# Two last stages of an attention and gated-layer kernel: an explicit order in place of a scheduler's

## The chip, the cores and the metric

The kernel runs on one core of a Trainium2 chip. The time is the device time of one execution in microseconds. Five engines work side by side, each through its own list of instructions: PE (the matrix engine; PEld is its loading of weights), DVE (vector), ACT (scalar), POOL (GpSimd) and SP (which issues DMA transfers). An instruction starts when its turn comes on its engine and what it waits for is there. PE writes its products into banks of an accumulator memory (PSUM), DVE and ACT read them from there.

## What is computed

```python
x = attention(q, k, v, cap)        # 4 x 12 heads, 448 tokens each: 1792 tokens x 768
h = ((x @ w1) * (x @ w2)) @ w3     # 1792 x 1024
x = h @ w_out                      # 1792 x 768
h = x @ w_in                       # 1792 x 1024
e = exp(h - max(h)); sm = e / (sum(e) + 1e-9)
solu = h * sm
ln = (solu - mean(solu)) / sqrt(var(solu) + 1e-6) * g_ln
out = ln @ w_out2                  # 1792 x 768
```

Everything is fp32, in and out.

## The kernel before

Attention comes first, then the gated stage. The plain products w3 · w_out · w_in are multiplied into one matrix W of 1024 x 1024 ahead of time, beside attention. So two matrix products are left behind the gated stage, and these are the two last stages: h = ab · W (ab are the gated values, kept in DRAM as `ab_dr`), and out = c · w_out2, where c is the normalised layer, kept in DRAM as `c_dr`, and g_ln is already multiplied into the weights.

Each stage goes over 7 pairs of 128-token tiles. For a pair and the weights cut into 2 x 2 blocks, seven block products take the place of eight, with sums of the blocks as operands; their order is 1, 2, 6, 7, 5, 4, 3. A product is 12 matmuls: 4 steps in depth times 3 terms, because every operand is kept as a rounded high part and a low part (`split`, L175: the high part is a cast on ACT, the low part a subtraction on DVE). A matmul is 512 columns wide in the first stage and 384 in the second.

The seven products of a pair go into three kinds of accumulator bank: u (two of them, in turn for successive pairs), y and v. Product 1 writes u, and its value is copied out (p1, ACT L774). Product 2 writes y, evicted with p1 added (DVE L781). Product 6 adds onto u, copied out (u2). Product 7 writes v, copied out (p7). Product 5 adds onto u, evicted with p7 added (L790). Product 4 adds onto v, evicted with u2 added (L793). Product 3 adds onto u, copied out by ACT (L795). So within a pair the third product needs the copy of the first, the fifth that of the third, the sixth that of the fourth, and the seventh the eviction behind the fifth.

Between the stages `solu` (L820 to 833) takes each tile of h through a maximum (DVE L823), an exponential with its sum (ACT L824), the weighting (DVE L827), squares with their sum (ACT L829), a power on POOL (L831) and the normalisation (DVE L832), and stores c. Behind it the second stage loads c again, transposed in blocks of 32 by the addresses of the DMA, turns it within the blocks (DVE L838, four times 512 a pair) and makes sums and operands of it (`turned_operands`, L840; x21 is a copy by ACT). The weights of the second stage are loaded into the place of the first stage's, behind their last products, and split in halves of 768 elements (`load_wg`, L868).

`ps`, `hp`, `op` and `conv` are pools; a tile with `bufs=n` has n places in turn, and a new tile waits until the one that had its place is no longer read. The order of instructions on each engine comes from the framework's scheduler, which works from estimated times; the loops at L875 to 915 say only what there is to do. The SoLU of the last pair is written behind the second pair of operands of the second stage.

Of the kernel before, what the change touches and what calls it, by code (L numbers as in the profile page):

```python
# [99 lines left out]
def attention_moe_solu(ctx: ExitStack, tc: tile.TileContext, q, k, v, cap, w12, w3t, wo, win, wout2, g_ln, out):  # L100
# [415 lines left out]
    def block_load(m, part, dr, t_dr, dst):  # L516
        sync.dma_start(out=raw(dst[:, 1, 2 * part:2 * part + 2, :]), in_=block_src(m, part, dr, t_dr))

    def block_split(dst, part):
        hi, lo = (dst[:, i, 2 * part:2 * part + 2, :] for i in range(2))  # L520
# [241 lines left out]
    NTT = NT // P  # L762
    PAIRS = NTT // 2

    def seven(n, a, wb, w, c1, c2, other):

        def product(bank, m, first):
            for k in range(NF // 2):
                for i, (x, e) in enumerate(THREE):
                    pe.matmul(bank, a[m][:, x, k * P:(k + 1) * P], wb[m][:, e, k, :], start=(first and k == 0 and i == 0), stop=(k == NF // 2 - 1 and i == 2), skip_group_check=not first)  # L770

        def kept(bank, name):
# [196 lines left out]
```

## Time and profile before

| | |
|---|---|
| device time, median of 3 runs | 824.34 us (822.47 to 825.29) |
| device time of the profiled execution | 828.39 us |
| its span, first to last instruction | 826.6 us |
| PE busy | 807.4 us, 98% |
| DVE busy | 604.3 us, 73% |
| ACT busy | 478.2 us, 58% |
| POOL busy | 74.8 us, 9% |
| first matmul of the two last stages | 574.75 us |

The profile is one execution, so sums are made against its own 828.39 us. A wait is written as idle time and the engine whose work ended it: `[1.02 <-ACT u L774]` behind a matmul means that PE stood still for 1.02 us until ACT's copy out of bank u at line 774 was done. Where several instructions of one line follow each other without a gap they stand as one (x12). PEclk is the granted clock of PE, 1.00 for full speed.

### The profile page before, as it was taken

How to read it: one execution, taken by the hardware profiler on the slowest of the kernel's cores; microseconds unless marked ns; L12 is line 12 of the kernel's file. 1: busy time of each engine (PE TensorE's matmuls, PEld its weight loads, DVE VectorE, ACT ScalarE, POOL GpSimd, SP SyncE). 2: the span in 40 equal slices, each digit the busy share in tenths (PEclk: the TensorE clock that was granted, in tenths of full speed). 3: DMA queues.
4: the chain of work that ended last, by engine and by line, in shares of the span. 5: the costliest groups of instructions: out<-in, count | busy, mean ns of one | idle time of the engine just before them, and what ended most of it. 6: DMA issues, size and time to landing. Idle time of an engine off the chain costs nothing. (4 is left out here: it accounts for less than half of the span.)

```text
span 826.6 us, 12057 instructions
## 1 busy us (share of the span) xinstructions
PE 807.4 (98%) x4251; PEld 676.4 (82%) x4251; DVE 604.3 (73%) x1076; ACT 478.2 (58%) x739; POOL 74.8 (9%) x147
## 2 busy tenths in 40 slices
PE   8999999999999999999989999999999999889998
PEld 4667888876777788888869999999888887789997
DVE  6999968788876687788746653332988889999851
ACT  6767868788677777777752301111655564754431
POOL 1110110110311221101111000000000000000000
PEclk9999999999999999999999999999999999889999
DMA  7878645577977445788546999971633349858411
GB/s 236 280 254 268 209 153 158 171 233 268 287 266 212 115 149 201 225 292 297 172 146 183 296 388 366 328 247 59 199 106 124 101 103 215 230 133 186 115 40 76
DMA packets 151292, 167.18 MB, mean 202 GB/s; under 512 B 71232, under 2 KB 124224, under 8 KB 149696
## 3 DMA queue, kind: packets, MB, share of 16 engines
q1 hardware_dynamic: 146240, 155.22, 59.0%
q0 software_dynamic: 4992, 11.19, 5.3%
q8 instruction: 33, 0.54, 0.3%
q14 instruction: 27, 0.22, 0.1%
HBM read 113.25 MB, written 47.53 MB: 195 GB/s over the span
## 5 line engine op out<-in xcount | busy, mean ns | idle before, releaser
L609 PE MATMUL ab<-xs,wt 128*128 128x448 f32 x1152 | 241.7, 367 | 0.4 <-ACT x L308 0.4
L609 PEld LDWEIGHTS ab<-xs,wt 128*128 128x128 f32 x1152 | 217.5, 189 | 20.6 <-ACT x L308 0.8
L259 ACT ACTIVATE sc<-sc,qscale 128x896 f32<-128x896 f32 (+1 forms) x96 | 84.9, 885 | 38.9 <-PE sc L251 28.6
L292 PE MATMUL o<-hi,v 128*66 128x448 f32 (+1 forms) x360 | 85.1, 371 | 1.8 <-ACT x L308 1.8
L260 ACT ACTIVATE p<-sc,capt 128x896 f32<-128x896 f32 (+1 forms) x96 | 85.6, 917 | 1.4
L770 PE MATMUL u<-ws,a 128*128 128x512 f32 x336 | 79.6, 390 | 1.0 <-ACT u L774 1.0
L380 PEld LDWEIGHTS f<-w,w_o 128*128 128x128 f32 x576 | 72.6, 190 | 9.4 <-issue 5.9
L380 PE MATMUL f<-w,w_o 128*128 128x256 f32 x576 | 78.4, 289 | 0.6 <-DVE w_o L177 0.6
L770 PEld LDWEIGHTS u<-ws,a 128*128 128x128 f32 x336 | 63.0, 188 | 14.3 <-ACT u L774 1.3
L275 DVE TENSOR_TENSOR lo<-p,hi 128x896 fp32r<-128x896 f32 x60 | 64.9, 1084 | 13.4 <-ACT hi L271 13.1
L398 PE MATMUL f<-w_i,w 128*128 128x512 f32 x288 | 70.1, 393 | 1.3 <-ACT w L176 1.0
L770 PE MATMUL u<-wg,c 128*128 128x384 f32 x336 | 64.3, 341 | 3.9 <-ACT h L795 3.9
L398 PEld LDWEIGHTS f<-w_i,w 128*128 128x128 f32 x288 | 53.7, 188 | 14.6 <-issue 1.5
L613 ACT COPY a<-ab 128x448 f32<-128x448 f32 x32 | 17.0, 532 | 82.9 <-PE ab L609 72.7
L770 PEld LDWEIGHTS u<-wg,c 128*128 128x128 f32 x336 | 60.3, 193 | 4.5 <-ACT h L795 4.2
L292 PEld LDWEIGHTS o<-hi,v 128*66 128x66 f32 (+1 forms) x360 | 39.1, 135 | 27.1 <-issue 8.8
L271 ACT CAST hi<-p 128x896 fp32r<-128x896 f32 x60 | 56.6, 948 | 0.4
L617 DVE TENSOR_TENSOR abs<-ab,a 128x448 f32<-128x448 f32 x32 | 19.8, 620 | 48.9 <-PE ab L609 36.5
L171 DVE SCALAR_TENSOR_TENSOR cv<-ld,cv 128x512 uint32<-128x512 uint32 (+1 forms) x80 | 51.9, 657 | 0.6
L172 DVE SCALAR_TENSOR_TENSOR cv<-ld,cv 128x512 uint32<-128x512 uint32 (+1 forms) x80 | 52.0, 656 | 0.6
L170 DVE TENSOR_SCALAR cv<-ld 128x512 uint32<-128x512 uint32 (+1 forms) x80 | 32.5, 410 | 20.5 <-DMA ld<-in_w 7.9
L309 POOL DMA_DIRECT2D xr<-x x48 | 25.6, 539 | 201.6 <-ACT x L308 194.5
(129 smaller groups left out, 1246.5 us busy)
## 6 DMA issues: line engine op xcount, KB each, us to landing
ld<-in_w SPq DMA_DIRECT2D x24, 512.0 KB, 5.0
w_dr<-wt SPq DMA_DIRECT2D x6, 1536.0 KB, 6.8
wt<-w_dr SPq DMA_DIRECT2D x6, 1536.0 KB, 8.4
ld<-in_w3t SPq DMA_DIRECT2D x16, 512.0 KB, 4.5
ab_dr<-abs SPq DMA_DIRECT2D x32, 224.0 KB, 4.9
ldab<-ab_dr SPq DMA_DIRECT2D x14, 512.0 KB, 4.0
c_dr<-e SPq DMA_DIRECT2D x14, 512.0 KB, 3.4
ldc<-c_dr SPq DMA_DIRECT2D x56, 128.0 KB, 3.3
```

The lines of the kernel that those rows point to most:

```text
L170: dve.tensor_scalar(x, hi, 5, 2, ALU.logical_shift_left, ALU.logical_shift_right)
L171: dve.scalar_tensor_tensor(x, hi, 0xC0000000, x, ALU.bitwise_and, ALU.bitwise_or)
L172: dve.scalar_tensor_tensor(x, lo, 29, x, ALU.logical_shift_right, ALU.bitwise_or)
L259: act.activation(sc[:, :w, :S], sc[:, :w, :S], AF.Tanh, scale=qscale)
L260: exp_[n, c] = act.activation(p, sc[:, :w, :S], AF.Exp, scale=capt)
L271: act.copy(hi, p)
L275: dve.tensor_tensor(lo, p, raw(hi), ALU.subtract)
L292: product_.append(pe.matmul(outs[n, j][:v_.shape[-1], :S], v_, t[rows, j if c < 3 else 0], **flags))
L380: pe.matmul(f[:, :QW], lw[:, a], rw[:, e], start=(g == 0 and m == 0), stop=(g == NF - 1 and m == 2))
L398: pe.matmul(f, w34[:, a, c, :], rw[:, e], start=(c == 0 and m == 0), stop=(c == NC - 1 and m == 2))
L609: pe.matmul(pp[f, b, i][:, :S], w[:, u], xs[b, c][:, e], start=(c == 0 and m == 0), stop=(c == NC - 1 and m == 2))
L770: pe.matmul(bank, a[m][:, x, k * P:(k + 1) * P], wb[m][:, e, k, :], start=(first and k == 0 and i == 0), stop=(k == NF // 2 - 1 and i == 2 ...
```

## The change

All of it is in the two last stages; in front of them the built program has the same instructions in the same order on every engine. The products, their order, their banks and their 12 matmuls stay. What is new:

- **The order.** Both stages are written under a mode in which the scheduler leaves the order alone. For pairs 0 to 13 (`r`; 0 to 6 are the first stage, 7 to 13 the second) and the seven products `j`, the program issues product (r, j), then the side work listed for the slot (r, j), then the eviction of product (r, j). Side work is listed by hand: operands, sums, transposes, SoLU's steps, weight splits, loads and stores.
- **Maxima in the evictions.** In the first stage the three evictions with a sum become one DVE instruction each that adds and takes a running maximum (L810), and product 3's copy moves from ACT to DVE and takes a maximum too (L830). SoLU's own pass for the maximum goes; a small negation (`top`, L836) is left.
- **Normalisation on ACT.** Instead of DVE's pass, an ACT pass with a scale and a shift per row (L859); POOL makes the shift with a second small product (L856).
- **Two low parts at once.** Operands 1 and 2, and 6 and 7, are cast and subtracted as one instruction of 1024 elements each (`two`), since their sources now lie beside each other. The transposes are 1024 wide as well, two a pair, into two banks each (L883).
- **Whole weights.** The second stage's weights are loaded and split as a whole (1536 elements), not in halves.
- **Places.** SoLU's last pair is spread over pairs 8 to 10. `early`, a pool that is closed ahead of the last stages, takes two tiles out of `conv`; `conv` and `op` hold four places for loads.

The core of the diff. The old functions that it removes are those printed above; of the lists of slots three lines stand here:

```diff
+    def at_slot(r, j, *todo):
+        side.setdefault((r, j), []).extend(todo)
...
+    def kept(r, g, name):
+        keeps[name] = hp.tile([P, HALF], F32, tag="kept", bufs=2, name=f"{name}_{r}")[:, :banks[g].shape[-1]]
+        act.copy(keeps[name], banks[g])
...
+    def added(r, i, half, g, keep):
+        w = banks[g].shape[-1]
+        dst = h[r][i][:, half * w:(half + 1) * w]
+        if r >= PAIRS:
+            dve.tensor_tensor(dst, banks[g], keeps[keep], ALU.add)
+            return
+        first = (i, half) in ((0, 0), (1, 1))
+        dve.tensor_tensor_reduce(dst, banks[g], keeps[keep], 1.0, LEAST if first else col(r, MAX, i), ALU.add, ALU.max, col(r, MAX if first else MOST, i))
...
+            dst = h[r][0][:, w:]
+            if r < PAIRS:
+                dve.tensor_scalar(dst, banks["u"], 0.0, col(r, MAX, 0), ALU.add, ALU.max, accum_out=col(r, MOST, 0))
+            else:
+                act.copy(dst, banks["u"])
...
+    def top(r):
+        dve.tensor_scalar(sts[r][:, NEG:NEG + 2], sts[r][:, MOST:MOST + 2], -1.0, None, ALU.mult)
...
+    def mean(r, i):
+        dve.tensor_scalar(col(r, MEAN, i), col(r, TOTAL, i), -1.0 / DF, None, ALU.mult)
...
+    def spread(r, i):
+        dve.tensor_scalar(col(r, VAR, i), col(r, SQUARES, i), 1.0 / DF, 1e-6, ALU.mult, ALU.add)
+        pool.tensor_tensor(col(r, RSTD, i), col(r, VAR, i), neghalf, ALU.pow)
+        pool.tensor_tensor(col(r, SHIFT, i), col(r, MEAN, i), col(r, RSTD, i), ALU.mult)
+
+    def normal(r, i):
+        act.activation(h[r][i], es[r, i], AF.Identity, bias=col(r, SHIFT, i), scale=col(r, RSTD, i))
...
+    def turn(r, i):
+        t = ps.tile([P, 2, HALF], F32, tag=f"t{i}", name=f"t{r}_{i}").rearrange("p a b -> p (a b)")
+        dve.transpose(t, x[r][i])
...
+    def two(r, ms, src):
+        t = op.tile([P, 2, 2, HALF], F32R, tag="two", bufs=3, name=f"a{r}_{ms[0]}{ms[1]}")
+        for i, m in enumerate(ms):
+            a.setdefault(r, {})[m] = t[:, i]
+        if src is not None:
+            split(t[:, :, 0], t[:, :, 1], src.rearrange("p (a b) -> p a b", a=2))
...
+    def sum1(r):
+        s = sums.setdefault(r, {})
+        s[1] = conv.tile([P, HALF], U32, tag="cv", bufs=2, name=f"s1_{r}").bitcast(F32)
+        a21 = quarter(r, 1, 0)
+        if r >= PAIRS:
+            a21 = s[0] = conv.tile([P, HALF], U32, tag="cv", bufs=2, name=f"x21_{r}").bitcast(F32)
+            act.copy(a21, quarter(r, 1, 0))
+        dve.tensor_tensor(s[1], quarter(r, 1, 1), a21, ALU.add)
...
+    def load_wg(m):
+        wg[m] = (wsp if m in EARLY[:4] else place["w5"] if m in EARLY else wsl).tile([P, 2, NF // 2, HALF], F32R, tag=f"w{m}", name=f"wg{m}")[:, :, :, :DM // 2]
+        block_load(m, None, G4, tg_dr, wg[m])
+
+    def split_wg(m):
+        block_split(wg[m], None)
...
+         (LAST, 4, split_wg, 1), (LAST, 5, split_wg, 2), (LAST, 6, split_wg, 6),
...
+    STEADY = ((-1, 2), (-1, 3), (-1, 3), (-1, 4), (-1, 4), (-1, 4), (-1, 5), (-1, 6), (0, 0), (0, 1))
...
+         (A + 2, 6, weigh, LAST, 0), (A + 3, 0, mean, LAST, 0), (A + 3, 0, squares, LAST, 0), (A + 3, 0, spread, LAST, 1), (A + 3, 1, spread, LAST, 0), (A + 3, 1, normal, LAST, 1),
...
+    with tc.manual_schedule():
+        for r in range(2 * PAIRS):
+            for j in range(len(ORDER)):
+                product(r, j)
+                for todo in side.pop((r, j), ()):
+                    todo()
+                evict(r, j)
+        for i in (1, 0):
+            give(2 * PAIRS - 1, i)
```

The same at three places of the built program. Names: `u_7`, `y_7`, `v_7` are banks of pair 7; `p1_7` is a kept copy; `a7_5` is operand 5 of pair 7, and `a9_67` operands 6 and 7 of pair 9 (before: `c0_5`, where c0 is the first pair of the second stage); `t` and `tp` are turned tiles, `ldc` and `ldx` loaded ones; `wg` are weights; `h`, `e` and `st` belong to SoLU. The number behind a name only tells tiles apart.

DVE in a late pair of the second stage, before: pair 11's evictions (o8, o9) with what stands between.

```order
L838 STREAM_TRANSPOSE tp6_1_8066<-ldc13_8013 128x512
L838 STREAM_TRANSPOSE tp6_2_8082<-ldc12_8008 128x512
L838 STREAM_TRANSPOSE tp6_3_8097<-ldc13_8013 128x512
L781 TENSOR_TENSOR o8_7868<-y_11_7871,p1_11_7885 128x384
L177 TENSOR_TENSOR c5_6_7991<-cs1_5_7978,c5_6_7991 128x512
L177 TENSOR_TENSOR c5_7_7995<-cs2_5_7979,c5_7_7995 128x512
L848 TENSOR_TENSOR cs0_6_8127<-tp6_3_8097,x21_6_8137 128x512
L177 TENSOR_TENSOR c5_5_7998<-cs0_5_7977,c5_5_7998 128x512
L177 TENSOR_TENSOR c5_4_8001<-tp5_3_7947,c5_4_8001 128x512
L790 TENSOR_TENSOR o9_7869<-u_11_7870,p7_11_7930 128x384
L177 TENSOR_TENSOR c5_3_8005<-cs3_5_7980,c5_3_8005 128x512
L793 TENSOR_TENSOR o9_7869<-v_11_7872,u2_11_7914 128x384
```

After, from pair 11's first eviction to its third:

```order
L807 TENSOR_TENSOR o11_0_7782<-y_11_7765,p1_11_7763 128x384
L883 STREAM_TRANSPOSE t12_0_7797<-ldx24_7581 128x1024
L178 TENSOR_TENSOR a12_12_7814<-t12_0_7797,a12_12_7814 128x2x512
L883 STREAM_TRANSPOSE t12_1_7817<-ldx25_7586 128x1024
L922 TENSOR_TENSOR s1_12_7833<-t12_1_7817,x21_12_7834 128x512
L927 TENSOR_TENSOR s2_12_7837<-s1_12_7833,t12_0_7797 128x512
L931 TENSOR_TENSOR s2_12_7837<-t12_0_7797,x21_12_7834 128x512
L807 TENSOR_TENSOR o11_1_7783<-u_11_7735,p7_11_7819 128x384
L178 TENSOR_TENSOR a12_67_7853<-s2_12_7837,a12_67_7853 128x2x512
```

Before, each eviction has one to five steps of 512 between it and the next, and transposes stand in front of the first eviction. After, both transposes of 1024, a low part of 1024 and three sums stand between the eviction of bank y and that of bank u.

ACT where the first stage passes into the second, before, up to the second pair's operands:

```order
L774 COPY p7_6_7107<-v_6_7049 128x512
L176 CAST c0_4_7183<-tp0_3_7124 128x512
L824 ACTIVATE e11_7023,st11_7022<-h11_6882,st11_7022 128x1024
L176 CAST wg6_7197<-wg6_7197 128x2x384 x2
L176 CAST c0_3_7187<-cs3_0_7162 128x512
L176 CAST c1_1_7355<-tp1_0_7274 128x512
L176 CAST wg7_7204<-wg7_7204 128x2x384 x2
L774 COPY p1_7_7259<-u_7_7244 128x384
```

After, the last entries ahead of the copy `p1_7`, which frees bank u of pair 7 for its third product:

```order
L177 CAST wg1_7026<-wg1_7026 128x4x384
L859 ACTIVATE h5_1_6866<-e5_1_7022,st5_6867 128x1024
L177 CAST wg2_7050<-wg2_7050 128x4x384
L859 ACTIVATE h5_0_6865<-e5_0_7044,st5_6867 128x1024
L177 CAST wg6_7075<-wg6_7075 128x4x384
L177 CAST a7_5_7145<-s1_7_6998 128x512
L177 CAST a7_4_7148<-t7_1_6952 128x512
L177 CAST a7_3_7167<-s2_7_7024 128x512
L177 CAST wg7_7096<-wg7_7096 128x4x384
L788 COPY p1_7_7174<-u_7_7153 128x384
```

The weights' casts have become whole, both normalisations of pair 5 stand between them, and four weights, two normalisations and three operands come ahead of that copy.

ACT in pair 9, before:

```order
L176 CAST c3_1_7681<-tp3_0_7600 128x512
L829 ACTIVATE h13_7046,st13_7395<-e13_7396,st13_7395 128x1024
L774 COPY p1_9_7585<-u_9_7570 128x384
L176 CAST c3_2_7684<-tp3_2_7632 128x512
L795 COPY o2_7418<-u_8_7420 128x384
L176 CAST c3_6_7691<-cs1_3_7678 128x512
L176 CAST c3_7_7695<-cs2_3_7679 128x512
```

After, with one of the last pair's two passes of squares (L851) ahead of the copy `u2_9`:

```order
L177 CAST a9_67_7446<-s2_9_7429 128x2x512
L788 COPY p1_9_7460<-u_9_7433 128x384
L177 CAST a9_5_7475<-s1_9_7425 128x512
L177 CAST a9_4_7497<-t9_1_7410 128x512
L851 ACTIVATE h6_1_7029,st6_7030<-e6_1_7333,st6_7030 128x1024
L788 COPY u2_9_7503<-u_9_7433 128x384
```

Before, one pass of squares (`L829 h13`) stands ahead of the copy `p1_9`; after, it is between `p1_9` and `u2_9`, behind two operands of 512.

## Rows read from the trace of the kernel before

**Rows 1.** Stretches: us, each engine's busy time (instructions), granted clock, DMA share, GB/s

```profile
574.80:699.90 125.10, 125.10 (x554) 103.56 (x553) 107.14 (x194) 71.45 (x123) 7.92 (x10) 1.00 0.48 135
699.90:735.00 35.10, 27.84 (x123) 25.37 (x122) 32.74 (x56) 23.54 (x40) 1.10 (x2) 0.87 0.77 191
735.00:822.60 87.60, 87.60 (x503) 87.31 (x502) 58.56 (x103) 35.29 (x69) 1.58 (x2) 0.99 0.41 112
```

**Rows 2.** PE's instructions in time: start, duration in us, then [idle before <-releaser]

```profile
577.49 2.88 PE L770 MATMUL y<-ws,a 128*128 128x512 f32 x12
580.21 2.88 PE L770 MATMUL u<-ws,a 128*128 128x512 f32 x12
...
702.84 3.02 PE L770 MATMUL u<-ws,a 128*128 128x512 f32 x12 [1.02 <-ACT u L774]
...
719.84 4.21 PE L770 MATMUL u<-wg,c 128*128 128x384 f32 x12 [3.90 <-ACT h L795]
...
731.35 3.27 PE L770 MATMUL y<-wg,c 128*128 128x384 f32 x12 [2.34 <-DVE o L781]
...
818.31 2.24 PE L770 MATMUL v<-wg,c 128*128 128x384 f32 x12
820.39 2.25 PE L770 MATMUL u<-wg,c 128*128 128x384 f32 x12
```

**Rows 3.** Stretches again: the first product after the longest wait

```profile
719.80:722.00 2.20, 2.17 (x7) 2.17 (x8) 2.20 (x4) 2.20 (x5) 0.00 (x0) 0.50 1.03 371
```

**Rows 4.** Groups of DVE's instructions, 600 to 827: busy us, mean ns | idle

```profile
L838 DVE STREAM_TRANSPOSE tp<-ldc 128x512 f32<-128x512 f32 x28 | 19.5, 711 | 2.0 <-DMA ldc<-c_dr 1.6 <-ACT x L847 0.2
...
L827 DVE SCALAR_TENSOR_TENSOR e<-e,st,h 128x1024 f32<-128x1024 f32 x14 | 17.8, 1278 | 0.0
L823 DVE TENSOR_REDUCE st<-h 128x1 f32<-128x1024 f32 x14 | 16.4, 1208 | 3.9 <-ACT h L795 3.9
L177 DVE TENSOR_TENSOR c<-tp,c 128x512 fp32r<-128x512 f32 x21 | 14.3, 681 | 4.2 <-ACT c L176 4.0
...
L177 DVE TENSOR_TENSOR wg<-wg 128x768 fp32r<-128x768 f32 x14 | 13.1, 943 | 1.3 <-ACT wg L176 1.3
L832 DVE TENSOR_SCALAR e<-e,st 128x1024 f32<-128x1024 f32 x14 | 11.2, 800 | 2.0 <-POOL st L831 1.9
...
L790 DVE TENSOR_TENSOR o<-u,p 128x384 f32<-128x384 f32 x7 | 3.9, 555 | 10.1 <-PE u L770 10.1
...
L826 DVE RECIPROCAL st<-st 128x1 f32<-128x1 f32 x14 | 2.1, 154 | 0.0
```

**Rows 5.** Groups of ACT's instructions, 600 to 827

```profile
L176 ACT CAST c<-cs 128x512 fp32r<-128x512 f32 x28 | 17.0, 621 | 9.1 <-PE u L770 8.1 <-PE v L770 1.0
L824 ACT ACTIVATE e<-h,st 128x1024 f32<-128x1024 f32 x14 | 16.1, 1153 | 8.1 <-DMA c_dr<-e 3.6 <-issue 2.9 <-DVE st L823 1.6
...
L176 ACT CAST c<-tp 128x512 fp32r<-128x512 f32 x21 | 12.4, 589 | 6.4 <-PE v L770 3.9 <-PE u L770 2.5
...
L176 ACT CAST wg<-wg 128x768 fp32r<-128x768 f32 x14 | 11.5, 836 | 12.5 <-DMA wg<-wg_dr 7.7 <-DMA wg<-tg_dr 4.8
...
L774 ACT COPY u<-u 128x384 f32<-128x384 f32 x7 | 3.4, 481 | 4.3 <-PE u L770 4.2
...
L824 ACT ACTIVATION_READ_ACCUMULATOR e<-h,st 128x1 f32 x14 | 2.6, 186 | 0.0
```

**Rows 6.** ACT's instructions in time: a 1024-wide cast

```profile
590.59 1.06 ACT L176 CAST ws<-ws 128x1024 fp32r<-128x1024 f32 x1
```

**Rows 7.** DVE's instructions in time: 1024-wide low parts

```profile
591.37 2.35 DVE L177 TENSOR_TENSOR ws<-ws 128x1024 fp32r<-128x1024 f32 x2
...
594.85 1.21 DVE L177 TENSOR_TENSOR ws<-ws 128x1024 fp32r<-128x1024 f32 x1
```

**Rows 8.** GpSimd's (POOL's) power, 600 to 827

```profile
L831 POOL TENSOR_TENSOR st<-st,neghalf 128x1 f32<-128x1 f32 x14 | 10.6, 760 | 283.0 <-DVE st L830 283.0
```

**Rows 9.** Landing of the first stage's two late weights

```profile
DMA to landing us min/median/max: 6.4/7.5/8.9
```

More of the change, by code (lines that the diff above doesn't have):

```diff
@@ L44 @@
 EARLY, LATE = (1, 2, 6, 7, 5), (4, 3)
+ORDER = EARLY + LATE
+LEAST = -3.0e38
 def raw(ap):
@@ L516, in block_load @@
     def block_load(m, part, dr, t_dr, dst):
[L517 removed]
+        sync.dma_start(out=raw(dst[:, 1, rows(part), :]), in_=block_src(m, part, dr, t_dr))
     def block_split(dst, part):
[L520 removed]
+        hi, lo = (dst[:, i, rows(part), :] for i in range(2))
         split(hi, lo, raw(lo))
@@ L761, in attention_moe_solu @@
     ps = ps_cm.__enter__()
[L762 to L772, printed above, removed]
-            t = hp.tile([P, HALF], F32, tag="kept", bufs=2, name=f"{name}_{n}")[:, :w]
-            act.copy(t, bank)
-            return t
-        u, y, v = (ps.tile([P, HALF], F32, tag=g, bufs=2 if g == "u" else 1, name=f"{g}_{n}")[:, :w] for g in ("u", "y", "v"))
-        product(u, 1, True)
-        p1 = kept(u, "p1")
-        product(y, 2, True)
-        dve.tensor_tensor(c1[:, :w], y, p1, ALU.add)
-        other(0)
-        product(u, 6, False)
-        u2 = kept(u, "u2")
-        other(1)
-        product(v, 7, True)
-        p7 = kept(v, "p7")
-        other(2)
-        product(u, 5, False)
-        dve.tensor_tensor(c2[:, w:], u, p7, ALU.add)
-        other(3)
-        product(v, 4, False)
-        dve.tensor_tensor(c2[:, :w], v, u2, ALU.add)
-        product(u, 3, False)
-        act.copy(c1[:, w:], u)
@@ L875, in attention_moe_solu, with product @@
-    for m in LATE:
+    PAIRS = NT // P // 2
+    LAST = PAIRS - 1
+    wg, banks, keeps, h, a, x, sums, es, sts = {}, {}, {}, {}, {0: begun}, {0: (lands.pop("x0"), lands.pop("x1"))}, {0: {}}, {}, {}
+    MAX, MOST, NEG, SUM, INV, TOTAL, MEAN, SQUARES, VAR, RSTD, SHIFT = range(0, 22, 2)
+    side, taken = {}, [2]
+    def at_slot(r, j, *todo):
+        side.setdefault((r, j), []).extend(todo)
+    def product(r, j):
+        m, w = ORDER[j], HALF if r < PAIRS else DM // 2
+        g, first = {1: "u", 2: "y", 6: "u", 7: "v", 5: "u", 4: "v", 3: "u"}[m], m in (1, 2, 7)
+        if first:
+            banks[g] = ps.tile([P, HALF], F32, tag=g, bufs=2 if g == "u" else 1, name=f"{g}_{r}")[:, :w]
+        b = ws if r < PAIRS else wg
+        for k in range(NF // 2):
+            for i, (p, e) in enumerate(THREE):
+                pe.matmul(banks[g], a[r][m][:, p, k * P:(k + 1) * P], b[m][:, e, k, :], start=(first and k == 0 and i == 0), stop=(k == NF // 2 - 1 and i == 2), skip_group_check=not first)
@@ new lines, in first_two, with second_two, one, fifth_one @@
+    def first_two(r):
+        two(r, (1, 2), x[r][0])
+    def second_two(r):
+        two(r, (6, 7), sums[r][2])
+    def one(r, m, src):
+        a[r][m] = t = op.tile([P, 2, HALF], F32R, tag="one", bufs=3, name=f"a{r}_{m}")
+        split(t[:, 0], t[:, 1], src)
+    def fifth_one(r):
+        one(r, 5, sums[r][1])
+    def fourth_one(r):
+        one(r, 4, quarter(r, 1, 1))
+    def third_one(r):
+        one(r, 3, sums[r][4])
+    def sum1(r):
[6 more added lines that the diff above has]
+        dve.tensor_tensor(s[1], quarter(r, 1, 1), a21, ALU.add)
@@ L916, in attention_moe_solu @@
+    assert not side
     ps_cm.__exit__(None, None, None)
```

256 lines of the change are left out of this document (137 added, 119 removed).

## The prediction

> **What bounds the kernel now.** I read the stretches first. From 574.8 to 822.6 us the engine that multiplies (PE) runs the two stages that the change rewrites, 98 products of 12 matmuls. In the first 125 us and in the last 88 us of it PE is never idle; only the passage from one stage to the other, 699.9 to 735, has PE busy for 27.84 of 35.10 us [rows 1]. So nothing can be won outside the passage, whatever is taken off the other engines. The list of PE's instructions gives the price of a product: starts lie 2.72 us apart where it is 512 wide and 2.08 where it is 384 wide [rows 2]. 49 of each make 133.3 + 101.9 = 235.2 us, and the stage takes 247.8: 12.6 us are lost today. 7.26 of these are three waits of 1.02, 3.90 and 2.34 us, the rest are matmuls at the lower of PE's two clocks behind the two longer waits: twelve of 384 took 4.21 us instead of 2.24 [rows 2], with a granted clock of 0.50, 1.2 GHz [rows 3]. In the same passage DVE is busy for 32.74 of 35.10 us [rows 1]: the splits of the second stage's weights, the late normalisation and the transposes meet there. **12.6 us are the most that the change can win.**
>
> **The change part by part.** *In front.* By the order of instructions nothing moves before the last products of the gated stage. The start at 574.8 stays, and so do the 4 us behind the last matmul.
>
> *Work removed and added.* Off DVE come 14 maxima of 1.21 us and 14 normalisations of 0.80 us, 28 us in all [rows 4]; onto ACT go 14 normalisations of 1024 elements. They are not shown in the trace in this form; bounds are a 1024-wide cast, 1.06 [rows 6], and the exponential with its accumulator read, 1.34 (1.153 in [rows 5] and some 0.19 for the read); I take 1.2, near the exponential, which also reads a value per row. The eviction that adds and takes a maximum at once is not shown either: between the plain eviction of 512, about 0.68 as the 512-wide low part, and that plus half a maximum, 1.28 [rows 4]; I take 0.78, near the first, since it reads each element once. In the first stage all of this lies beside PE, which does not wait there today, so it wins nothing there by itself.
>
> The trace has the normalisation at 0.80 us on DVE and a pass of ACT over the same 1024 elements at 1.15 [rows 4, 5]. The Trainium skill, "ScalarE: Activation LUTs", Rules for kernel authors, says that adds and multiplies belong on VectorE, which speaks against this move. By that rule the two places below where PE waits for ACT behind a normalisation, 0.9 us and 1.2 of the passage, would go, and DVE's chains would get 0.8 longer each: no different sum.
>
> *The new order and its price.* Every engine now works through a list, and side work stands ahead of the eviction of the product beside which it was put. PE needs an accumulator bank back at fixed points: the third product waits for the copy of the first, the fifth for that of the third, the seventh for the sum that evicts the fifth. If side work in front of that copy waits or is long, PE waits. I add up, along each list, what stands between the product that starts it and the copy that PE needs. Dependent steps cost their whole duration, independent ones that follow each other some 0.07 less (2.35 for two of 1.21 [rows 7]). Sizes not in the trace follow from two rows: a 1024-wide transpose 0.71 + 0.53 = 1.24, a 1024-wide cast out of PSUM 0.59 + 0.43 = 1.02, a whole weight split 1.48 on ACT and 1.74 on DVE (the 768-wide ones of 0.84 and 0.94, lengthened by 768 elements) [rows 4 to 7].
>
> (a) Pairs 0 and 1. The last two weights land 6.4 to 8.9 us after their issue at about 576 to 577.5 [rows 9], before ACT comes to them. From the third product's end ACT and DVE do the copy, two operands with their sum, three weight casts, one copy, the last low part and the eviction: 0.59 + 0.62 + 0.68 + 0.68 + 0.52 + 0.95 + 0.5 + 0.95 + 1.06 + 1.21 + 0.78 = 8.5, against three products, 8.16. With the copies queued behind it 1.0 us (0 to 3).
>
> (b) Pair 6 into 7. From the fourth product's end: low part of two operands and the mean 1.35, squares 1.15, cast of the first weight 1.48, its low part 1.74, eviction 0.78: 6.5 against two products, 5.44, so 1.1 us. Behind that: a small step 0.15, GpSimd's power 0.76 [rows 8] and its product, not shown, 0.1 to 0.76 (I take 0.76, the nearest), normalisation 1.2, third weight 1.48 + 1.74, two low parts 1.2, a sum 0.6, a cast 0.62, fourth weight 1.48, and only then the copy of pair 7's first product, 0.48: 10.5. In all 17.0, against 3 x 2.72 + 2 x 2.08 = 12.3. PE is late by 4.7.
>
> (c) Pairs 7 and 8. Four weight low parts on DVE make the seventh product late by 0.35. Then from its start: cast, low part, eviction, transpose, copy, three sums, a small step, cast, low part: 0.55 + 1.21 + 0.5 + 1.24 + 0.59 + 2.04 + 0.15 + 1.06 + 1.21 = 8.55, against 3 x 2.08 and the 0.35 until the third matmul, 6.6: 1.9.
>
> (d) Pair 9. Operands 6 and 7 come after a chain of 11.5 (copy and cast 1.03, low part 0.68, transpose, cast, low part, transpose 4.7, copy 0.59, three sums 2.04, cast and low part 2.27, some 0.2 of evictions between) against 5 x 2.08 + 0.35 = 10.75: 0.9. The weighting of pair 6 (small steps of 0.15 and 1.28) and the squares stand ahead of the copy that frees the bank for the fifth product: 0.6 + 0.4 + 1.3 + 0.5 + 0.6 + 0.6 + 0.2 + 1.15 + 0.48 = 5.8 against 3.9: 1.9. Its eviction then comes 6.4 behind that copy, against 4.16: 2.2.
>
> (e) Pair 10. The same three places: squares ahead of the first copy 2.3, a normalisation ahead of the next 0.9, the chain of (f) begun late 2.4.
>
> (f) Pairs 11 and 12, where no side work is left but their own. From the third product's end to the sum that evicts the fifth: copy 0.48, cast 1.02, low part 1.21, transpose 1.24, copy 0.59, three sums 2.04, eviction 0.55, together 7.1 against three products, 6.24 [rows 2, 4, 5]: 0.9 to 1.0 each, 2.0. Today PE waits nowhere from 735 on.
>
> Sum: 1.0 + 4.7 + 2.25 + 5.0 + 5.6 + 2.0 = 20.6 us. Five per cent on every step is 0.35 at each of 14 late points: 15.6 to 25.6. *The clock.* Today's waits of 3.90 and 2.34 us bring 5.3 us of lower clock (12.6 less 7.26); the change has one of 3.5 and three of 2.2 to 2.4. That costs 0 to 6; while PE is slow the late engines catch up, so I take 2. Loss after: 22.6, today 12.6: **10 us slower**. Against the profiled execution that is 828.4 + 10 = 838.4; the median of the runs shown, 824.3, lies 4 us under it, so 834.4.
>
> **Rivals.** *The lists keep pace behind the passage (faster).* If the chain of (f) is under 6.24 us, links some 12% shorter than their rows, and the side work of (d) and (e) falls into the room that this leaves, only (a), (b) and (c) are left, 8.0 us: 824.3 - 4.6 = 819.7. For it: maxima and normalisation leave DVE, 28 us. Against it: the late points hang on order, not on DVE's total, and the rows used agree among themselves to a few hundredths. 0.11.
>
> *Even.* The late points cost about 12.6, as if two thirds of them were met: 824. 0.08.
>
> *Slower still.* The new eviction needs 1.3 us and stands three times in every pair, 0.5 more at five late points of (a) and (b), and all four long waits bring the lower clock, 6: 20.6 + 2.5 + 6 - 12.6 = 16.5, 841. 0.16.
>
> *The change doesn't do what it says.* The order of the built program shows the lists as written, so this has no share of its own.
>
> **How the numbers follow.** The forecast has 0.65, 834.4 with 830 to 839 as its own range. 0.3% is 2.5 us, about what a measurement of this kernel can tell from no change. Faster 0.11, same 0.08, slower 0.65 + 0.16 = 0.81. From 15.6 without the clock, 827, to 25.6 with 5.5 for the clock, 843, I expect 8 in 10.
>
> **What would show it.** After the change PE should be without waits from pair 2 to pair 6's sixth product; wait about 1 us there and 3 to 4 us for the copy of pair 7's first product; then wait at two or three products of each of pairs 8 to 10, for ACT's copies and DVE's eviction, and about 1 us once in each of pairs 11 and 12, released by DVE. DVE should be less busy in all and PE's idle time about 20 us. If PE runs through pairs 11 and 12 without a wait, the sum along the lists is wrong, and with it the sign.

## The result, and the profile after

The changed kernel takes 838.23 us (median of 4 runs, 836.71 to 841.7), the kernel before in the same series 824.82 (822.47 to 828.0): a ratio of 1.0131, interval 1.0088 to 1.0173. It is slower, by about 10.8 us going by the ratio; the ratio's interval allows 7 to 14 us, and the two medians lie 13.4 us apart. 834.4 was predicted, 827 to 843 as the range.

All comparisons below rest on two kinds of number. The ratio to the kernel before, with its interval, comes from timed runs. **Gaps** come from one profile: the distances between the starts of successive products, less 2.72 us for each of 512 and 2.08 for each of 384, added up over the 98 products. They hold PE's waits and its slow matmuls. Each kernel was profiled once, so how much its gaps vary between executions isn't known. The kernel before has 12.5 us of gaps, the changed one 21.8. The profiled executions lie 8.3 us apart (828.39 and 836.71): 9.2 more gaps, and a first product at 573.87, 0.9 us earlier than before.

The stretches of the changed kernel answer to [rows 1]; the columns are the same (PE, PEld, DVE, ACT, POOL busy, granted clock, DMA share, GB/s). 573.9 to 704 is the first stage without its last products, 704 to 740 the passage, then pairs 9 and 10, then pairs 11 to 13:

```profile
573.90:704.00 130.10, 129.60 (x571) 106.77 (x570) 94.11 (x199) 83.81 (x121) 13.33 (x22) 1.00 0.49 142
704.00:740.00 36.00, 30.12 (x155) 28.03 (x155) 27.34 (x33) 21.39 (x28) 2.35 (x2) 0.95 0.80 195
740.00:787.00 47.00, 40.05 (x214) 38.14 (x213) 34.43 (x53) 21.11 (x34) 1.95 (x4) 0.96 0.57 125
787.00:831.00 44.00, 42.38 (x242) 41.42 (x240) 24.51 (x33) 13.96 (x24) 0.00 (x0) 1.00 0.15 59
```

Before, PE was idle in the passage alone. Now it also stands still for 7 of the 47 us of pairs 9 and 10, and 1.6 us behind them, while in the second stage DVE is busy for 76% of the passage and less later, and ACT for less than DVE throughout. So neither of the engines that PE waits for is full.

PE's products with a wait of over 0.6 us, and one slow one without (774.92), in the order of time (start, duration, then idle time and releaser); they answer to [rows 2]:

```profile
706.65 3.02 PE L784 MATMUL u<-ws,a 128*128 128x512 f32 x12 [1.07 <-DVE st L810]
...
717.92 3.72 PE L784 MATMUL u<-wg,a 128*128 128x384 f32 x12 [4.06 <-ACT p L788]
...
735.50 2.00 PE L784 MATMUL u<-wg,a 128*128 128x384 f32 x10 [0.64 <-DVE a L178]
...
756.66 2.35 PE L784 MATMUL u<-wg,a 128*128 128x384 f32 x12 [1.46 <-ACT u L788]
...
762.99 4.44 PE L784 MATMUL u<-wg,a 128*128 128x384 f32 x24 [1.90 <-DVE o L807]
...
771.45 3.68 PE L784 MATMUL u<-wg,a 128*128 128x384 f32 x12 [1.94 <-ACT p L788]
774.92 2.56 PE L784 MATMUL v<-wg,a 128*128 128x384 f32 x12
...
782.80 4.43 PE L784 MATMUL u<-wg,a 128*128 128x384 f32 x24 [1.15 <-DVE o L807]
...
798.43 4.43 PE L784 MATMUL u<-wg,a 128*128 128x384 f32 x24 [0.80 <-DVE o L807]
...
814.07 4.43 PE L784 MATMUL u<-wg,a 128*128 128x384 f32 x24 [0.80 <-DVE o L807]
```

The first is pair 6's last product, the second pair 7's third; then pair 8's third, pair 9's fifth and last, pair 10's third and last, and the last of pairs 11 and 12. Slow are three: 3.72, 3.68 and 2.56 instead of 2.24. The steps that the prediction had to estimate are in the groups of the same trace (mean ns behind the comma):

```profile
L178 DVE TENSOR_TENSOR wg<-wg 128x1536 fp32r<-128x1536 f32 x7 | 12.3, 1758 | 6.5 <-ACT wg L177 6.4
...
L810 DVE CUSTOM_DVE_ANT_0 h<-v,u,st 128x512 f32<-128x512 f32 x7 | 5.2, 743 | 0.5 <-PE v L784 0.4
...
L810 DVE CUSTOM_DVE_ANT_0 h<-u,p 128x512 f32<-128x512 f32 x7 | 4.8, 688 | 3.3 <-issue 2.3 <-ACT h L851 1.0
```

```profile
L859 ACT ACTIVATE h<-e,st 128x1024 f32<-128x1024 f32 x14 | 17.4, 1245 | 8.9 <-POOL st L856 8.7
...
L177 ACT CAST wg<-wg 128x1536 fp32r<-128x1536 f32 x7 | 10.2, 1469 | 0.0
```

The eviction that adds and takes a maximum at once costs 0.69 us for banks u and y, as much as a plain step of 512 (0.68 in [rows 4]), and 0.74 for bank v; behind each stands a read of the accumulator of 0.08, so 0.77 to 0.83 in all, where 0.78 was taken. The normalisation on ACT takes 1.25 (1.2 was taken), a whole weight 1.47 on ACT and 1.76 on DVE (1.48 and 1.74), a 1024-wide transpose 1.25 (1.24). On POOL means say little: the power takes 0.55 to 2.16 us (0.80 in the mean), the second product 0.19 to 1.17 (0.46; 0.76 was taken).

Why a copy comes late is best seen on ACT in pair 9, ahead of the copy that frees bank u for the fifth product:

```profile
750.58 0.59 ACT L177 CAST a<-t 128x512 fp32r<-128x512 f32 x1
755.00 1.15 ACT L851 ACTIVATE h<-e,st 128x1024 f32<-128x1024 f32 x1 [3.83 <-DVE st L848]
...
756.15 0.46 ACT L788 COPY u<-u 128x384 f32<-128x384 f32 x1
```

ACT stands still for 3.83 us, because the squares wait for DVE's mean. The copy of 0.46 us stands behind them. What it copies was complete at 753.1 (ten matmuls from 751.10, 2.01 us), and the bank is free only at 756.6. Here a waiting instruction holds up all that stands behind it on its engine. In the passage the two engines wait for each other in turn:

```profile
709.20 1.25 ACT L859 ACTIVATE h<-e,st 128x1024 f32<-128x1024 f32 x1 [2.50 <-POOL st L856]
710.35 1.46 ACT L177 CAST wg<-wg 128x1536 fp32r<-128x1536 f32 x1
...
715.50 0.62 ACT L177 CAST a<-s 128x512 fp32r<-128x512 f32 x1 [2.68 <-DVE s L936]
716.02 1.47 ACT L177 CAST wg<-wg 128x1536 fp32r<-128x1536 f32 x1
717.39 0.47 ACT L788 COPY p<-u 128x384 f32<-128x384 f32 x1
```

```profile
706.74 2.16 POOL L855 TENSOR_TENSOR st<-st,neghalf 128x1 f32<-128x1 f32 x1 [4.22 <-DVE st L854]
708.98 0.19 POOL L856 TENSOR_TENSOR st<-st 128x1 f32<-128x1 f32 x1
```

A normalisation of pair 5 holds ACT up for 2.50 us behind POOL's shift, and nearly all of that is the power of 2.16 us; the third weight's cast starts late for it; DVE's low part of that weight and a sum come late in turn, and ACT waits 2.68 us for the sum (L936). The copy that PE needs comes last in ACT's list here, at 717.39.

### The profile page after: what moved, and what is told of

The parts are those of the page before. It is cut to its first block, busy times and chain, and to the rows that moved or that the text cites. A ratio compares the mean times of both kernels' runs of the same rounds, so it can differ in the third digit from the quotient of the medians.

```text
span 834.9 us, 11954 instructions
## 1 busy us (share of the span) xinstructions
PE 808.9 (97%) x4251; PEld 673.9 (81%) x4251; DVE 586.7 (70%) x1043; ACT 488.4 (58%) x713; POOL 82.5 (10%) x161
## 4 chain that ended last, share of the span: by engine, by line
PE 69%; DVE 12%; DMA 8%; ACT 6%; issue 4%; POOL 1%; SPq 0%; POOLq 0%; DVEq 0%; ACTq 0%
PE ab L614 25%; PE u L784 11%; PE o L293 9%; PE f L400 6%; PE f L382 5%; PE v L784 4%; PE sc L252 4%; PE y L784 3%; DMA wg_dr<-wg 2%; ACT a L177 1%; DVE t L883 1%; PE sc L248 1%; DVE cv L172 1%; DVE cv L173 1%; DMA ld<-in_w3t 1%
## 5 line engine op out<-in xcount | busy, mean ns | idle before, releaser
L784 PE MATMUL u<-wg,a 128*128 128x384 f32 x336 | 66.0, 348 | 13.4 <-ACT p L788 6.2
L784 PEld LDWEIGHTS u<-wg,a 128*128 128x128 f32 x336 | 60.5, 195 | 17.0 <-ACT p L788 7.2
L178 DVE TENSOR_TENSOR a<-s,a 128x512 fp32r<-128x512 f32 (+1 forms) x43 | 36.5, 852 | 22.6 <-ACT a L177 22.1
L177 ACT CAST a<-s 128x512 fp32r<-128x512 f32 (+1 forms) x43 | 31.6, 745 | 33.5 <-DVE s L931 14.8
L622 DVE TENSOR_TENSOR abs<-ab,a 128x448 f32<-128x448 f32 x32 | 19.9, 621 | 44.4 <-PE ab L614 27.3
```

Of the source, the lines that this page charges most:

```text
L177: act.copy(th, x)
L784: pe.matmul(banks[g], a[r][m][:, p, k * P:(k + 1) * P], b[m][:, e, k, :], start=(first and k == 0 and i == 0), stop=(k == NF // 2 - 1 and ...
```

## The experiments

Each kernel is the changed one with the edit shown, or, from e9 on, that of e8. The table stands ahead, so that the sections can be short. The last column is the difference of the ratios to the changed kernel's 1.0131, times 825 us.

| kernel | median us | ratio to before (interval) | gaps us | against the changed kernel, us: gaps, ratio |
|---|---|---|---|---|
| changed | 838.23 | 1.0131 (1.0088 to 1.0173) | 21.8 | |
| e1_scheduled | 825.12 | 1.0001 (0.9984 to 1.0019) | 11.5 | -10.2, -10.7 |
| e2_sums_behind | 833.19 | 1.0100 (1.0071 to 1.0129) | 18.4 | -3.4, -2.6 |
| e3_norm_later | 832.71 | 1.0089 (1.0068 to 1.0109) | 20.0 | -1.8, -3.5 |
| e4_no_late_solu | 830.63 | 1.0070 (1.0049 to 1.0090) | 15.8 | -6.0, -5.0 |
| e5_norm_dve | 837.18 | 1.0119 (1.0081 to 1.0158) | 20.8 | -0.9, -1.0 |
| e6_evict_first | 835.48 | 1.0104 (1.0070 to 1.0138) | 20.9 | -0.9, -2.2 |
| e7_half | 840.84 | 1.0181 (1.0135 to 1.0228) | 24.3 | +2.5, +4.1 |
| e8_reordered | 819.51 | 0.9909 (0.9880 to 0.9939) | 2.6 | -19.2, -18.3 |
| e9_old_work | 825.00 | 0.9988 (0.9967 to 1.0009) | 9.1 | -12.7, -11.8 |
| e10_old_own_order | 817.13 | 0.9894 (0.9861 to 0.9927) | 1.8 | -19.9, -19.6 |

The ratios' intervals are 0.4 to 0.9% wide, 3 to 8 us, so steps of 1 to 4 us are told by the gaps of one profile each, above all by the single waits that an edit was to move, and the ratio only says that nothing else moved by much.

**e1: the same work, ordered by the scheduler.**

```diff
-    with tc.manual_schedule():
+    with nullcontext():
         for r in range(2 * PAIRS):
```

> The changed kernel with one edit: its two last stages are not held in the written order, the scheduler orders them as it did before. The work stays: maxima in the evictions, normalisation on ACT, two low parts at once, 1024-wide transposes, whole weights. Theory (the loss is the written order): PE loses about what it lost before, 9 to 13 us in these two stages, and the time is 821 to 828. Rival (the loss is the work that was moved or widened, ACT's normalisation above all): PE still waits some 20 us and the time stays at 834 to 841. Half of each would be 829 to 833.

825.12, level with the kernel before, and 11.5 us of gaps against its 12.5. In the scheduler's order the new work is neither dear nor of use: the change's whole loss is gone. The scheduler also put products of the second stage between the last ones of the first (`wg` among `ws`), and was left with one long wait in the passage, for DVE's eviction. PE's products, as above:

```profile
699.73 1.15 PE L784 MATMUL y<-wg,a 128*128 128x384 f32 x5 [1.18 <-DVE wg L178]
700.72 2.96 PE L784 MATMUL u<-ws,a 128*128 128x512 f32 x12
...
729.92 6.83 PE L784 MATMUL u<-wg,a 128*128 128x384 f32 x24 [5.85 <-DVE o L807]
```

**e2: three sums behind the eviction, in pairs 10 to 12.** The slots of sum1 to sum3 for the next pair go from the fifth product to the sixth.

```diff
-    STEADY = ((-1, 2), (-1, 3), (-1, 3), (-1, 4), (-1, 4), (-1, 4), (-1, 5), (-1, 6), (0, 0), (0, 1))
+    STEADY = ((-1, 2), (-1, 3), (-1, 3), (-1, 5), (-1, 5), (-1, 5), (-1, 5), (-1, 6), (0, 0), (0, 1))
```

> One edit: in pairs 10, 11 and 12 the three sums for the next pair stand behind DVE's eviction of bank u (the fifth product's) instead of ahead of it. Theory (a late point is a sum along the list between a product and the eviction that it needs): the waits of 1.15, 0.80 and 0.80 us behind that eviction go, with the gaps around them 3.6 us, nothing new comes, since operands 6 and 7 have more than two products of room: 3.6 us less, 834.6 (833.5 to 836). Rival (the chain only moves): operands 6 and 7 become late at the next pair's third product by as much, the time stays within 1.5 us of 838.2.

The gaps at the last products of pairs 10, 11 and 12 (1.32, 0.96, 0.97 and what follows each) go without a trace, 3.4 us in all; the time came out a little under the range. DVE in pair 11 and PE's product behind it, which was that with 0.80 us of wait:

```profile
793.17 1.25 DVE L883 STREAM_TRANSPOSE t<-ldx 128x1024 f32<-128x1024 f32 x1
794.82 0.56 DVE L807 TENSOR_TENSOR o<-u,p 128x384 f32<-128x384 f32 x1 [0.40 <-issue]
795.29 0.68 DVE L922 TENSOR_TENSOR s<-t,x 128x512 f32<-128x512 f32 x1
```

```profile
796.64 4.32 PE L784 MATMUL u<-wg,a 128*128 128x384 f32 x24
```

The eviction (0.56) now starts when its product is done, ahead of the sums, and PE's 24 matmuls at 796.64 have no wait. The next pair's operands 6 and 7 are still in time, so the chain did not merely move.

**e3: pair 5's normalisations out of the passage.**

```diff
-                 (r, 4, mean, n, 0), (r, 4, squares, n, 0), (r, 4, spread, n, 1), (r, 5, spread, n, 0), (r, 5, normal, n, 1), (r, 6, normal, n, 0), (r, 6, store, n, 1), (r + 1, 0, store, n, 0))
+                 (r, 4, mean, n, 0), (r, 4, squares, n, 0), (r, 4, spread, n, 1), (r, 5, spread, n, 0), *(((r, 5, normal, n, 1), (r, 6, normal, n, 0), (r, 6, store, n, 1), (r + 1, 0, store, n, 0)) if r < LAST else ((r + 1, 4, normal, n, 1), (r + 1, 5, normal, n, 0), (r + 1, 5, store, n, 1), (r + 1, 6, store, n, 0))))
```

> One edit: the two normalisations of pair 5, which stand between the weights' casts on ACT in pair 6, come in pair 7 behind the copy that PE waits for, with their stores. Theory (the passage holds more work than three products of room): the wait of 4.06 us for the copy of pair 7's first product falls to about 2, and the slow stretch behind it (1.48) goes or shrinks: 2 to 3.5 us less, 835 to 836. Rival (the wait is the weights' chain alone, DVE's low parts set the pace and ACT's passes are hidden behind them): the wait stays over 3.5, and the time within 1 us of 838.2.

The wait of 4.06 us falls to 1.13, further than expected, and the slow stretch behind it goes; the time lies 2 us under the forecast range. But only 1.8 us of gaps are won: at pair 8's third product 0.6 us come back, and behind two later waits PE is slow, where it was not before:

```profile
714.48 2.35 PE L784 MATMUL u<-wg,a 128*128 128x384 f32 x12 [1.13 <-ACT p L788]
...
759.12 6.03 PE L784 MATMUL u<-wg,a 128*128 128x384 f32 x24 [1.90 <-DVE o L807]
...
767.59 2.35 PE L784 MATMUL u<-wg,a 128*128 128x384 f32 x12 [0.35 <-ACT p L788]
...
772.46 2.38 PE L784 MATMUL u<-wg,a 128*128 128x384 f32 x12 [0.44 <-ACT u L788]
...
778.94 6.03 PE L784 MATMUL u<-wg,a 128*128 128x384 f32 x24 [2.01 <-DVE o L807]
```

```profile
761.20:763.20 2.00, 2.00 (x8) 2.00 (x7) 1.35 (x3) 1.38 (x2) 0.00 (x0) 0.50 0.99 154
```

The 24 matmuls at 759.12 took 6.03 us, behind a wait of 1.90, and from 761.20 to 763.20 the granted clock was 0.50 (1.2 GHz); in the changed kernel the same 24, behind the same wait of 1.90, took 4.44 at full clock (762.99 above). So the cause of most of the long wait is shown: the normalisations among the casts, the second of which waits for POOL. What such a repair wins in all isn't, since waits and slow stretches elsewhere shift with it.

**e4: no SoLU for the last pair** (its steps in pairs 8 to 10 left out, h stored as it is).

```diff
-    plan((A + 1, 0, top, LAST), (A + 1, 1, exponential, LAST, 1), (A + 1, 2, exponential, LAST, 0), (A + 2, 1, weigh, LAST, 1), (A + 2, 2, mean, LAST, 1), (A + 2, 2, squares, LAST, 1),
-         (A + 2, 6, weigh, LAST, 0), (A + 3, 0, mean, LAST, 0), (A + 3, 0, squares, LAST, 0), (A + 3, 0, spread, LAST, 1), (A + 3, 1, spread, LAST, 0), (A + 3, 1, normal, LAST, 1),
-         (A + 3, 2, normal, LAST, 0), (A + 3, 2, store, LAST, 1), (A + 3, 3, store, LAST, 0))
+    plan((A + 3, 2, store, LAST, 1), (A + 3, 3, store, LAST, 0))
```

> The changed kernel without SoLU for the last pair: its maximum, exponentials, weighting, squares, powers and normalisations in pairs 8 to 10 of the second stage are left out, h is stored as it is. Theory (in pairs 9 and 10 PE waits because this work stands ahead of copies and evictions): the waits of 1.46 (fifth product of pair 9) and 1.94 (third of pair 10) go, that of 1.90 falls to about 0.9, the slow stretches behind the second (1.7) go; 6 to 7.5 us less, 831 to 832.5. Those of pairs 6 to 8, 11 and 12 stay as they are. Rival (the operands' chains are too long by themselves): the waits of pairs 9 and 10 stay at over half, under 3.5 us less.

6.0 us fewer gaps, although the slow stretch behind pair 7's long wait, which the edit does not touch, came out at 2.8 us and not 1.5. The waits of 1.46 and 1.94 in pairs 9 and 10 are gone, that of 1.90 falls to 0.66, that at pair 10's last product stays (1.19, before 1.15), as do the short ones at pair 9's third. So of the four long waits of (d) and (e) two were this side work, and a third was so in the main; the fourth is the sums of e2.

**e5: normalisation back on DVE.**

```diff
-        act.activation(h[r][i], es[r, i], AF.Identity, bias=col(r, SHIFT, i), scale=col(r, RSTD, i))
+        dve.tensor_scalar(h[r][i], es[r, i], col(r, MEAN, i), col(r, RSTD, i), ALU.add, ALU.mult)
```

> The changed kernel with one edit: the normalisation goes back from ACT to DVE (0.80 us for 1024 elements there), in the same slots; POOL's second product is left in place and has no reader. Theory (places and chains set the end, not which engine does it, as the prediction says: ACT's lists get 1.2 shorter at two late points, DVE's 0.8 longer): the waits move by under 1 us each, the time within 2 us of 838.2. Rival (ACT's pass, 1.25 us, is what PE waits for in the passage and in pair 10): the wait of 4.06 us in pair 7 falls by over 1.5 and the time by 3 or more.

0.9 us fewer gaps, 837.18. One wait moved by more than expected, that of 4.06 to 2.57, just at the rival's mark of 1.5: ACT's casts no longer stand behind a wait for POOL. The slow product behind it stayed (1.67), the other waits moved by under 0.4, and the time did not fall by the rival's 3. The Trainium skill, "ScalarE: Activation LUTs", Rules for kernel authors, puts adds and multiplies on VectorE; the trace agrees on the step, 0.80 us there against 1.25. In the time it is worth about 1 us in this order, which these intervals can't tell from nothing; "no different sum" was near enough.

**e6: evictions ahead of side work in the whole second stage.**

```diff
                 product(r, j)
+                if r >= PAIRS:
+                    evict(r, j)
                 for todo in side.pop((r, j), ()):
                     todo()
-                evict(r, j)
+                if r < PAIRS:
+                    evict(r, j)
```

> One edit: in the second stage (pairs 7 to 13) the eviction of each product is written ahead of the side work of its slot, not behind it. Rival, the simple reading of the prediction (PE waits because side work stands in front of copies): the waits for ACT's copies and DVE's evictions in pairs 7 to 12 go, some 14 us, and the time falls to 822 to 827. Theory (the chains themselves are late, an operand that gives way to a copy is then late for its own product): waits for copies give way to waits for operands, releasers turn from copies to casts and low parts; 0 to 4 us less, 834 to 838.

20.9 us of gaps, where 21.8 were. PE's waits by releaser (us in total, times, longest), of the changed kernel and then of e6:

```profile
PE u L784 <- ACT p L788: 6.2, 3, 4.1
PE u L784 <- DVE o L807: 4.7, 4, 1.9
...
PE u L784 <- ACT u L788: 1.5, 1, 1.5
PE u L784 <- DVE a L178: 0.9, 2, 0.6
```

```profile
PE u L784 <- DVE o L807: 2.4, 4, 1.4
PE u L784 <- DVE a L178: 2.4, 4, 0.6
PE u L784 <- ACT a L177: 1.7, 2, 0.8
PE v L784 <- ACT wg L177: 1.6, 1, 1.6
PE u L784 <- ACT u L788: 1.4, 1, 1.4
PE v L784 <- DVE wg L178: 1.3, 1, 1.3
...
PE u L784 <- ACT p L788: 0.6, 1, 0.6
PE v L784 <- ACT p L788: 0.6, 1, 0.6
```

Waits for copies (`p`, `u`) and evictions (`o`) shrink from 12.4 to 5.0 us, and waits for operands and weights (`a`, `wg`) grow from 0.9 to 7.0. A rule for where an eviction stands does not help by itself: what gives way to it must have room.

**e7: halves.** Operands 1 and 2, 6 and 7 by two casts and two low parts, transposes in two halves.

```diff
-            split(t[:, :, 0], t[:, :, 1], src.rearrange("p (a b) -> p a b", a=2))
+            for i in range(2):
+                split(t[:, i, 0], t[:, i, 1], src[:, i * HALF:(i + 1) * HALF])
...
-        dve.transpose(t, x[r][i])
+        for k in range(2):
+            dve.transpose(t[:, k * HALF:(k + 1) * HALF], x[r][i][:, k * HALF:(k + 1) * HALF])
```

> One edit in two places: operands 1 and 2, and 6 and 7, are cast and subtracted as two instructions of 512 each on ACT and DVE in turn, and the transposes are halves of 512, in the same slots. Theory (width is no cause; one instruction more costs some 0.2 us per chain for two transposes): 0 to 3 us more, 838 to 841, the waits of pairs 11 and 12 grow from 0.80 to 1.0 to 1.5. Rival (two low parts at once lengthen the chains, since the first half waits for the second): 3 or more less.

2.5 us more gaps; the waits of pairs 11 and 12 grow from 0.80 to 1.41. Two steps at once are a small gain, not the loss. The Trainium skill, "Perfetto Trace Analysis", Optimizing Scalar/DVE Operations, says that where these engines make others wait without being full, "breaking up instructions may allow work to be completed sooner"; here that is the case (DVE busy 27.34 of 36 us in the passage), and it did not.

**e8: the same instructions in another order.** One list of all steps takes the place of the slots. It was found by adding up the durations of the changed kernel's trace along the lists for many orders, each one step away from the last, and keeping what made PE wait less. Pair 0 is left as it was. Two rows of the list, a product first, then what is issued behind it (`E` an eviction):

```diff
+P:7:1 E:7:1 load_wg:3 split_wg:5 normal:5:1 spread:5:0
...
+P:9:5 first_two:10 fifth_one:10 sum3:10 weigh:6:1
...
+        for step in STEPS.split():
+            f, *args = step.split(":")
+            does[f](*map(int, args))
```

> The changed kernel, the same instructions, in another written order from pair 1 on (pair 0 stays): one list of all steps, in which evictions stand where their product ends, chains of operands begin earlier, pair 5's normalisations lie in pair 7 and the last pair's SoLU lies in gaps of pairs 8 to 11. Durations of the changed kernel's trace, added up along these lists, leave PE 1 us of waits, that of pair 0. Theory (the loss is the order, the work itself fits beside PE): gaps of 1 to 3 us in place of 21.8, so 838.2 less 19 to 21, 817 to 820, under the kernel before. Rival (the passage holds too much work for any order, or the loads of weights and of c come too late): over 6 us stay, 823 or more.

819.51, ratio 0.9909 (0.9880 to 0.9939), 2.6 us of gaps: as the theory says, and 0.9% faster than the kernel before. Its stretches:

```profile
575.60:700.00 124.40, 123.90 (x546) 102.06 (x545) 92.55 (x195) 79.17 (x115) 10.30 (x20) 1.00 0.47 137
700.00:736.00 36.00, 35.19 (x189) 33.05 (x188) 32.26 (x44) 25.45 (x34) 1.48 (x4) 1.00 0.85 222
736.00:813.50 77.50, 77.45 (x446) 76.83 (x444) 54.71 (x81) 34.46 (x57) 1.82 (x4) 1.00 0.47 112
```

PE is busy for 35.19 of 36 us in the passage, with DVE at 32.26 and ACT at 25.45, and the granted clock is 1.00 in every stretch. So the passage is not too full for the right order. Two waits are left, at pair 0 (0.50) and pair 7 (0.81).

**e9 and e10: is the moved work what makes that order possible?** e9 keeps e8's order and takes the cheaper work back: plain evictions, a pass of DVE for each maximum, the normalisation on DVE. e10 gives this old work an order of its own, found in the same way.

```diff
-        dve.tensor_scalar(sts[r][:, NEG:NEG + 2], sts[r][:, MOST:MOST + 2], -1.0, None, ALU.mult)
+        for i in (1, 0):
+            dve.tensor_reduce(col(r, NEG, i), h[r][i], axis=AX.X, op=ALU.max, negate=True)
...
-        act.activation(h[r][i], es[r, i], AF.Identity, bias=col(r, SHIFT, i), scale=col(r, RSTD, i))
+        dve.tensor_scalar(h[r][i], es[r, i], col(r, MEAN, i), col(r, RSTD, i), ALU.add, ALU.mult)
```

> The kernel of e8 in its written order, with the change's cheaper work taken back: plain evictions, an own pass for each maximum on DVE (1.21 us, at the place of the small negation), product 3's copy on ACT, the normalisation on DVE (0.80). The wide steps and whole weights stay. What it asks: does the moved work pay once the order is right? If the 28 us of DVE that the change saves are what the order of e8 lives on, passes of 1.21 us at places meant for 0.16 make products late in most pairs: durations added up along the lists give some 10 us of gaps, 826 to 829. If they lie in room that PE does not need, 0 to 2 more gaps and 819.5 to 822.

> The same old work (own passes for the maxima, normalisation on DVE) in a written order made for it, from pair 1 on. Theory (in these stages the order is what sets the time, and the work moved off DVE only widens the room): durations added up along the lists give 1 us of waits, so gaps of 1 to 4 us, 817 to 821, level with e8. Rival (DVE holds too much in the passage, so without the moved work no order gets through): over 6 us of gaps, 823 or more.

e9 has 9.1 us of gaps, near the 10 that the sum along the lists gave (the time, 825.0, is 1 us under its range): an order is made for its work. e10 has 1.8 and takes 817.13, ratio 0.9894 (0.9861 to 0.9927), level with e8:

```profile
575.00:700.00 125.00, 124.51 (x550) 102.83 (x549) 107.56 (x181) 71.07 (x111) 10.21 (x20) 1.00 0.49 134
700.00:736.00 36.00, 35.63 (x191) 33.29 (x190) 34.08 (x40) 23.27 (x32) 1.48 (x4) 1.00 0.86 230
736.00:813.00 77.00, 76.29 (x441) 75.96 (x439) 56.18 (x83) 33.65 (x57) 1.43 (x4) 1.00 0.45 113
```

DVE is busy for 34.08 of 36 us in the passage and 18 us more than in e8 over the two stages (197.8 against 179.5), and PE still loses next to nothing. The 28 us of passes that the change takes off DVE are thus about 18 net: product 3's copy (0.75 a pair), the reads of the accumulator and the negations come onto it. Taking maxima in the evictions and moving the normalisation are worth nothing that these runs can tell, once the order is right.

## Why the prediction was right, point by point

| place | forecast gaps | measured |
|---|---|---|
| (a) pairs 0 and 1 | 1.0 | 1.0 |
| (b) pair 6 into 7 | 4.7 | 5.6 |
| (c) pairs 7 and 8 | 2.25 | 1.3 |
| (d) pair 9 | 5.0 | 5.0 |
| (e) pair 10 | 5.6 | 3.5 |
| (f) pairs 11 and 12 | 2.0 | 2.1 |
| lower clock | 2 | 3.2 |
| sum | 22.6 | 21.8 |

**Direction and mechanism.** The forecast was that side work ahead of a copy makes PE wait at fixed points, and named them. Nearly every named place has its wait, with the named releaser: ACT's copy in pair 7 (4.06, forecast 3.6 behind the 1.1 of pair 6), ACT's copy and DVE's eviction in pairs 9 and 10, DVE's eviction in 11 and 12. Pairs 2 to 5 have none. Pair 8 differs: the signs named two or three late products there, for copies and evictions, and only its third is late, for an operand's low part, as the sum of (c) has it. e2 and e4 take two of the causes away, and what they explain goes: 3.4 and 6.0 us. e6 says what the sums are about: with every eviction of the second stage ahead of its side work the gaps stay (20.9 us), because operands come late instead. What makes PE wait is the length of a whole list with its waits, and not the place of the eviction alone.

**Terms that were mis-sized.** (b): 0.9 too little, and it lies on one step. POOL's power and its product were taken as 0.76 each, 1.52 together; from the power's start at 706.74 to the normalisation's at 709.20 the trace has 2.46, since the power took 2.16 us there. The power at this place took 2.0 us or more in e2, e3, e4, e6 and e7 too, and 0.55 in e8 and e10, where it comes at another time. DVE runs the low part of a weight beside it (1.76 us from 706.73); whether that is why, no run here was made for.

(c): the four low parts on DVE, counted as 0.35 at pair 7's last product, cost nothing there, and pair 8 was 1.3 late, not 1.9. (e): 2.1 too much; the second place of it, ACT's normalisation ahead of the next copy, had no wait, and the chain of (f) came 1.3 late in pair 10, not 2.4. Both lie behind slow products of PE, which give the other engines time to catch up, as the prediction says of slow stretches in general: 1.5 us ahead of (c), 1.7 within (e) (3.68 and 2.56 us). Other runs bear this out. In e4 the slow products ahead of (c) cost 2.8 us, and pair 8 is only 0.7 late. In e3, whose edit leaves pair 10 alone, no product is slow between pair 10's third and last: its fifth then waits 0.44 us for ACT's copy, and its last comes 2.2 late.

The other steps shown above were right to a few hundredths. In (d) the first place is given as 0.9, where its own terms make 0.75 (11.5 less 10.75). The lower clock cost 3.2 us, more than the 2 taken and inside 0 to 6. The places miss by up to 2.1 us with both signs, so 21.8 against 22.6 is in part luck: without the clock 20.6 was forecast, and 18.6 came.

**The step from the profile to the median.** +10 was forecast for the gaps and +9.2 came. The predicted 834.4 is nevertheless 3.8 under the median of 838.23. The prediction took off 4 us, as the profiled execution before lay that much above its median; the changed kernel's profiled execution lies 1.5 under its own. Half a microsecond is the kernel before itself, whose median is 824.82 in the series with the changed one. In the profiles shown here the first product of these stages starts anywhere from 570.96 (e1) to 575.57 (e8), so executions differ by some us ahead of the change. What the rest of the 3.8 is made of can't be told from one profile each.

**The bound.** "12.6 us are the most that the change can win" held: e8 and e10 win 9.9 and 10.7 in gaps, 7.5 and 8.7 us by their ratios. The rival "the lists keep pace behind the passage" needed links 12% shorter than their rows; they were as in their rows, and of the 28 us off DVE that spoke for it 18 are net. The rival "slower still" needed 1.3 us for the new eviction; it takes 0.77 to 0.83 with its read.

## What to carry to other kernels

A written order is priced by adding up, on each engine, what stands between the product that starts a list and the copy that the next product needs, with the waits of what stands ahead of that copy; with durations from rows, such sums gave 20.6 us of waits where 18.6 came, missed single places by up to 2.1, and found an order that wins. An engine's share of busy time says little about it: 18 us less on DVE changed nothing, and three sums moved behind one eviction won 3.4 us. Mending one wait moves others, so an order is searched as a whole, for the work that it is to hold.

## What was not expected of the hardware

Taking a maximum along with the addition in an eviction cost little: 0.69 us against 0.68 for a plain step, or 0.74 in bank v's, which carries a maximum on, with 0.08 for reading the accumulator. A power of one column on POOL took 0.55 us in some places and 2.16 in another, and there ACT and PE waited for it. And the lower clock does not follow from the length of one wait: behind the same 1.90 us the same 24 matmuls ran at full clock in the changed kernel (4.44 us) and partly at half in e3 (6.03). What decided it is open; no run here was made for it.
